# Retention followed by a low-rank mixer: the recurrent state in 64-token steps, on quarter tiles of the TensorE array

## The chip, the cores and the metric

The kernel runs on one core of a Trainium2 chip. A core has a TensorE (PE, matrix multiply; its weight loads are listed as PEld), a VectorE (DVE), a ScalarE (ACT), a GpSimd (POOL) and a SyncE (SP), each with its own queue of instructions, and 16 DMA engines. Matrix products land in PSUM, which VectorE and ScalarE read; everything else lives in SBUF. The metric is the time of one execution on the device in microseconds (us).

## What is computed

Inputs: q, k, v of shape (8 batches, 8 heads, 576 tokens, 64), and the weights of a mixer. The computation, cut to what matters:

```
scores = q @ k^T / sqrt(64)                      # per batch and head, 576 x 576
ret    = scores * gamma_h^(i-j)  for j <= i, else 0
attn   = ret @ v                                 # (8, 8, 576, 64)
x      = attn, heads side by side                # (8, 576, 512)
h      = (x^T @ U @ V)^T                         # U: 576 x 32, V: 32 x 576, along the tokens
u      = x + h
out    = u + relu(u @ w_ch1) @ w_ch2             # 512 -> 2048 -> 512
```

Since gamma^(i-j) = gamma^i * gamma^-j, the kernel scales v's rows by gamma^-j beforehand and the result's rows by gamma^i afterwards. What is between is causal linear attention: within a block of tokens masked scores times v, and for everything earlier q times a running state S, the sum of k^T v over earlier tokens (a 64x64 matrix for each head).

## The kernel before

**Pairs and chunks.** Batches are taken in four pairs (`pr`). The 1152 tokens of a pair make nine chunks of 128 (`NI = 9`); chunk `J = 4` holds the last 64 tokens of the even batch in partitions 0 to 63 and the first 64 of the odd batch in partitions 64 to 127. The first pair has code of its own (`startup`, `first_stretch`, functions ending in `_u` and `_J`), which the change leaves alone but for two memsets. "Later pairs" are pairs 1 to 3.

**One chunk.** q and k come by DMA as float32 (`load`), are cast to bf16 (`cast_qk`: k on VectorE at L244, q on ACT at L246), v is scaled on POOL (`scale_v`, L255), and SP issues a DMA that transposes q and k (`xbar`, L263); casts, scaling and transpose together are `prep`. The attention of a chunk is

- `SC`: eight matmuls k^T q of 64 rows by 128 columns, one for each head, into the PSUM tile psc (two banks; the two heads of a pair stand in different banks);
- `mask`: one VectorE multiply of psc by a triangle, to ret in SBUF (L286);
- `RV`: eight matmuls ret times v into po (two banks); `QS`: eight matmuls q times the state (64 rows), added into po;
- `XS`: one VectorE multiply of po by gamma^i, to x (L326);
- `ST`: four matmuls k^T v, which add to the state that stays in the PSUM tile pss; `Scopy`: one ACT copy of it to bf16 (s_sb, L349), which the next chunk's QS reads.

In `attn_items` a chunk makes two items: A (SC, QS, mask) and Bf (RV, XS, ST, Scopy). The odd batch of a pair starts with an item of its own, SJ, for the state of chunk J's second half.

**The order.** The whole program is in an order written out by hand: each engine gets its instructions as the Python code issues them. The main work of a batch is `y1_items` (L481: 16 feature tiles of u @ w_ch1, four matmuls for each PSUM tile, and after each tile a Relu on ACT at L486 that takes it to SBUF) and then `y2_items` (L515: for each chunk 16 matmuls into one PSUM tile, then the add of u on VectorE at L504 and a store). For an even batch (`par = 0`, four chunks) a Y1 item is one tile of 512 columns; for an odd one (five chunks) it is two tiles, of 384 and 256 columns. In the odd batch of the first pair the two are 512 and 128. All these tiles, and those of Y2, go round the three buffers of `ps_big`.

`merge` goes through the main items, whose costs it knows, and puts the items of two fills between them at equal distances: the attention of the next batch and its mixer (`attn_items` + `mixer_items`) over the first 0.82 of the main cost, and the loads and preps (`aux_items`) over the first 0.62 or 0.58. In the loop b is the batch whose main work runs: with b even (2, 4, 6) the fill is the odd batch of the same pair, with b odd (3, 5) the even batch of the next pair, and the last batch (b = 7) has none. A first merge, ahead of the loop, runs what is left of batch 1's Y1 and the Y2 of batches 0 and 1, and fills in pair 1's even batch.

[...]

Of the kernel before, what the change touches and what calls it, by code (L numbers as in the profile page):

```python
# [9 lines left out]
FP32 = mybir.dt.float32  # L10
BF16 = mybir.dt.bfloat16
AF = mybir.ActivationFunctionType
ALU = mybir.AluOpType


def merge(main, *fills, leads=(0.82, 0.64)):

    total = sum(c for c, _ in main)
    queues = []
    for fill, lead in zip(fills, leads):  # L20
        n = len(fill)
        queues.append([((k + 0.5) / n * lead * total, fn) for k, fn in enumerate(fill)])
    done = 0.0
    for cost, fn in main:
        for q in queues:
            while q and q[0][0] <= done:
                q.pop(0)[1]()
        fn()
        done += cost
    for q in queues:  # L30
        for _, fn in q:
            fn()


@with_exitstack
def kernel(
# [11 lines left out]
    nc = tc.nc  # L48

    B, H, S, D = q.shape  # L50
# [9 lines left out]
    J = 4  # L60
# [28 lines left out]

    ident = consts.tile([P, P], BF16, name="ident")  # L90
    tri = consts.tile([P, P], BF16, name="tri")
    triJ = consts.tile([P, P], BF16, name="triJ")
    triU = consts.tile([P, 2, P], BF16, name="triU")
    iotaU = consts.tile([P, 2, P], FP32, name="iotaU")
    posU = consts.tile([P, 4, 2, H], FP32, name="posU")
# [18 lines left out]
    def early_consts():  # L114
        make_identity(nc, ident)
        nc.gpsimd.memset(lnb, math.log(scale))
        nc.gpsimd.iota(
            posU, pattern=[[2 * P, 4], [1, 2], [0, H]], base=0, channel_multiplier=2,
            allow_small_or_imprecise_dtypes=True,
        )  # L120
        nc.gpsimd.iota(
            iotaU, pattern=[[-1, 2], [1, P]], base=0, channel_multiplier=-2,
            allow_small_or_imprecise_dtypes=True,
        )
        nc.gpsimd.iota(
            pos, pattern=[[P, NI], [0, H]], base=0, channel_multiplier=1,
            allow_small_or_imprecise_dtypes=True,
        )
        make_upper_triangular(nc, tri, val=1.0, diag=True)
        for h in range(H):  # L130
            nc.vector.memset(lngt[:, :, h], lng[h])
        nc.vector.tensor_scalar_add(posU[:, 2:4], posU[:, 2:4], -float(4 * P - HALF))
        nc.vector.tensor_tensor(
            out=posU.rearrange("p u j h -> p (u j) h"),
            in0=lngt[:, 0:8, :], in1=posU.rearrange("p u j h -> p (u j) h"), op=ALU.mult)
        nc.scalar.activation(out=vscaleU, in_=posU, func=AF.Exp, bias=lnb, scale=-1.0)
        nc.vector.tensor_scalar(
            out=triU[0:HALF], in0=iotaU[0:HALF], scalar1=0.0, scalar2=None, op0=ALU.is_ge)
        nc.vector.tensor_scalar(
            out=triU[HALF:P], in0=iotaU[HALF:P], scalar1=-float(P), scalar2=None,  # L140
            op0=ALU.is_ge)
        nc.vector.tensor_scalar_add(pos[:, J + 1:NI, :], pos[:, J + 1:NI, :], -float(S))
        nc.vector.tensor_scalar_add(pos[HALF:P, J, :], pos[HALF:P, J, :], -float(S))
        nc.vector.tensor_tensor(out=lngt, in0=lngt, in1=pos, op=ALU.mult)
        nc.scalar.activation(out=qscale, in_=lngt, func=AF.Exp, bias=0.0, scale=1.0)
        nc.scalar.activation(out=vscale, in_=lngt, func=AF.Exp, bias=lnb, scale=-1.0)
        nc.vector.tensor_copy(out=triJ, in_=tri)
        nc.vector.memset(triJ[0:HALF, HALF:P], 0.0)
        nc.vector.memset(U_E[:, J, :], 0.0)
        nc.vector.memset(U_O[0:HALF, 0, :], 0.0)  # L150
        nc.vector.tensor_copy(out=fan, in_=ident[0:R, None, 0:R].to_broadcast([R, 4, R]))
        nc.vector.tensor_copy(out=swap[:, 0:HALF], in_=ident[:, HALF:P])
        nc.vector.tensor_copy(out=swap[:, HALF:P], in_=ident[:, 0:HALF])
        nc.vector.memset(V4[:, 0:HALF], 0.0)
        nc.vector.memset(V4[:, HALF + S:], 0.0)
        nc.vector.memset(sblk, 0.0)
# [109 lines left out]

    st = {}

    def SC(pr, i):
        c = ch[pr, i]  # L270
        qkT = c["qkT"]
        psc = ps_sc.tile([P, 2, NHP, P], FP32, tag="psc", name="psc")
        for hp in range(NHP):
            for hl in range(2):
                r = slice(hl * HALF, (hl + 1) * HALF)
                nc.tensor.matmul(  # L276
                    psc[:, hl, hp, :], qkT[r, NHP + hp, :], qkT[r, hp, :],
                    start=True, stop=True,
                )
        c["psc"] = psc  # L280

    def mask(pr, i):
        c = ch[pr, i]
        ret = ret_pool.tile([P, H, P], BF16, tag="ret", name="ret")
        m = triJ if i == J else tri
        nc.vector.tensor_tensor(  # L286
            out=ret.rearrange("p (hp hl) i -> p hl hp i", hl=2), in0=c["psc"],
            in1=m[:, None, None, :].to_broadcast([P, 2, NHP, P]), op=ALU.mult,
        )
        c["ret"] = ret  # L290

    def QS(pr, i):
        c = ch[pr, i]
        if "po" not in c:
            c["po"] = ps_o.tile([P, 2, dm], FP32, tag="po", name="po")
        s_sb = st["s_sb"]
        m = slice(0, HALF) if i == J else slice(0, P)
        for hp in range(NHP):
            for hl in range(2):
                r = slice(hl * HALF, (hl + 1) * HALF)  # L300
                nc.tensor.matmul(  # L301
                    c["po"][m, hl, hp * D:(hp + 1) * D],
                    c["qkT"][r, hp, m], s_sb[r, hp, hl * D:(hl + 1) * D],
                    start=(i != J and hp == 0), stop=True, skip_group_check=True,
                )

    def RV(pr, i):
        c = ch[pr, i]
        if "po" not in c:
            c["po"] = ps_o.tile([P, 2, dm], FP32, tag="po", name="po")  # L310
        first = i in (0, J)
        for hp in range(NHP):
            for hl in range(2):
                h = 2 * hp + hl
                nc.tensor.matmul(  # L315
                    c["po"][:, hl, hp * D:(hp + 1) * D],
                    c["ret"][:, h, :], c["v"][:, h, :],
                    start=(first and hp == 0), stop=True, skip_group_check=True,
                )

    def XS(pr, i):
        c = ch[pr, i]
# [8 lines left out]
            op=ALU.mult,  # L331
        )

    def ST(pr, i):
        c = ch[pr, i]
        if i in (0, J):
            st["S"] = ps_s.tile([P, NHP, P], FP32, tag="pss", name="pss")
        rows = slice(HALF, P) if i == J else slice(0, P)
        vf = c["v"].rearrange("p h d -> p (h d)")
        for hp in range(NHP):  # L340
            nc.tensor.matmul(  # L341
                st["S"][:, hp, :],
                c["qk"][rows, 1, hp * P:(hp + 1) * P], vf[rows, hp * P:(hp + 1) * P],
                start=(i in (0, J) and hp == 0), stop=True, skip_group_check=True,
            )

    def Scopy(pr, i):
        s_sb = s_pool.tile([P, NHP, P], BF16, tag="s_sb", name="s_sb")
        nc.scalar.activation(out=s_sb, in_=st["S"], func=AF.Copy)  # L349
        st["s_sb"] = s_sb  # L350

    def attn_items(pr, par):
        items = []

        def A(i):
            SC(pr, i)
            if i not in (0, J):
                QS(pr, i)
            mask(pr, i)

        def Bf(i):
            RV(pr, i)
            if i == J:
                QS(pr, i)
            XS(pr, i)
            if i not in (J, NI - 1):
                ST(pr, i)
                Scopy(pr, i)

        def SJ():  # L370
            ST(pr, J)
            Scopy(pr, J)

        if par == 1:
            items.append(SJ)
        for i in (range(0, J + 1) if par == 0 else range(J + 1, NI)):
            items.append(lambda i=i: A(i))
            items.append(lambda i=i: Bf(i))
        return items

    def mixer_items(pr, par, split=False):
# [514 lines left out]
    def first_stretch():  # L896
# [58 lines left out]
        unit(3, (2, 3), True)  # L955
        load_w2(0)
        load_w2(2)
        xT = [None] * NCC

        def to_xT(ccs, chunks):  # L960
# [43 lines left out]
            Y1(f, 1)  # L1004
        return rest[6:]

    def idle():
        pass

    with tc.manual_schedule():  # L1010
        early_consts()
        startup()
# [8 lines left out]
        for b in range(2, B):  # L1021
            pr, par = divmod(b, 2)
            fill = []
            if b + 1 < B:
                fill = attn_items((b + 1) // 2, (b + 1) % 2) + mixer_items(
                    (b + 1) // 2, (b + 1) % 2)
            n = 5 if b % 2 == 1 else 4
            aux = aux_items(g, g + n)
            g += n
            merge(y1_items(par) + y2_items(pr, par), fill, aux, leads=(0.82, 0.58))  # L1030

# [1 line left out]
_INS = ['q', 'k', 'v', 'moe_U', 'moe_V', 'moe_w_ch1', 'moe_w_ch2']  # L1033
# [26 lines left out]
```

## Time and profile before

| what | us |
|---|---|
| median of three runs | 333.81 (332.57 to 334.24) |
| the profiled execution's own time | 332.29 |
| its span, first to last instruction | 330.5 |
| its busy time on PE / DVE / ACT / POOL | 317.6 / 136.4 / 136.9 / 77.8 |
| L481 and L515, the main matmuls | 135.8 and 124.5 busy |
| L486, the Relus | 89.6 busy |
| L286, L326, L349: mask, XS, state copy | 29.4, 18.6, 14.3 busy |
| TensorE's granted clock | 1.000 |

How to read the lines. A line of the groups names source line, engine, operation, output<-input, shapes and count; then busy us and mean ns of one; then the idle time of the engine just ahead of these instructions and what ended it. A timeline line gives start and length in us, engine, line, operation, and in brackets the idle time before it. A line of the chain of waits in order of time gives start, length and what the end of the program waited for there, merged over neighbouring instructions of the same line ("x8"). [...]

### The profile page before, as it was taken

The numbers are of one execution on the slowest core, as the hardware profiler recorded it, in microseconds if no ns is written. First come the engines' busy times: TensorE is split into PE (matmuls) and PEld (weight loads), VectorE is DVE, ScalarE is ACT, GpSimd is POOL, SyncE is SP. The second block draws the span as 40 slices with busy tenths as digits, with TensorE's granted clock in tenths as the row PEclk, the third lists the DMA queues.
The fourth block names the chain that finished last, engine by engine and source line by source line (L and its number), as shares of the span: only waits on it lengthen the run. The fifth ranks groups of instructions, "written<-read, shape, count | busy, mean of one in ns | idle before, by whom it ended". The sixth has DMA issues, their size and how long they took to land.

```text
span 330.5 us, 7031 instructions
## 1 busy us (share of the span) xinstructions
PE 317.6 (96%) x2942; PEld 174.0 (53%) x2964; DVE 136.4 (41%) x193; ACT 136.9 (41%) x289; POOL 77.8 (24%) x112
## 2 busy tenths in 40 slices
PE   7899999999999999999999999999999996999996
PEld 2464554555444455467644454467644453467544
DVE  5383554444534254534334354534534342510022
ACT  2547656772200573057700573067700662037400
POOL 5675636022221311131121311131211300110000
DMA  7999999999999399949995499959995011330012
GB/s 210 236 226 257 231 196 191 184 171 198 239 238 193 101 226 172 217 125 170 189 251 136 110 218 181 205 135 193 196 211 158 32 34 33 102 106 2 0 70 91
DMA packets 151311, 53.17 MB, mean 161 GB/s; under 512 B 131984, under 2 KB 148752, under 8 KB 151280
## 3 DMA queue, kind: packets, MB, share of 16 engines
q1 hardware_dynamic: 144512, 40.40, 68.0%
q0 software_dynamic: 6768, 12.32, 14.9%
q8 instruction: 23, 0.38, 0.6%
q14 instruction: 8, 0.07, 0.1%
HBM read 36.85 MB, written 9.44 MB: 140 GB/s over the span
## 4 chain that ended last, share of the span: by engine, by line
PE 91%; DMA 3%; DVE 2%; issue 1%; SPq 1%; ACT 1%; POOL 0%
PE ps_y L481 38%; PE ps_y L515 37%; PE psc L276 3%; DMA stage_t<-in_q_dram 2%; PE po L315 2%; PE pss L341 2%; PE pss L691 1%; SPq L578 1%; PE ph L422 1%; PE ps_y L526 1%; PE pa L395 1%; PE po L301 1%; DMA qkT<-qk 1%; DVE xt L682 1%; PE po L665 1%
## 5 line engine op out<-in xcount | busy, mean ns | idle before, releaser
L481 PE MATMUL ps_y<-uT,w_sb 128*128 128x512 bf16 (+3 forms) x768 | 135.8, 326 | 0.4 <-DVE uT L702 0.4
L486 ACT ACTIVATE y<-ps_y 128x384 bf16<-128x384 f32 (+2 forms) x192 | 89.6, 489 | 112.2 <-PE ps_y L481 111.6
L515 PE MATMUL ps_y<-w_sb,y 128*128 128x512 bf16 x538 | 124.5, 379 | 1.5 <-issue 0.8
L481 PEld LDWEIGHTS <-w_sb 128*128 128x128 bf16 x768 | 69.2, 98 | 47.4 <-issue 1.4
L515 PEld LDWEIGHTS <-y 128*128 128x128 bf16 x560 | 52.2, 98 | 59.8
L504 DVE TENSOR_TENSOR o_sb<-ps_y,u 128x512 f32<-128x512 f32 (+2 forms) x38 | 25.2, 663 | 81.5 <-PE ps_y L515 79.3
L255 POOL TENSOR_TENSOR vt<-stage_t,vscale 128x512 bf16<-128x512 f32 (+1 forms) x29 | 30.2, 1049 | 85.2 <-DMA stage_t<-in_v_dram 74.4
L286 DVE TENSOR_TENSOR ret<-psc,tri 128x1024 bf16<-128x1024 f32 x24 | 29.4, 1224 | 44.1 <-PE psc L276 44.1
L507 POOL DMA_DIRECT2D out_dram<-o_sb x31 | 17.2, 554 | 117.5 <-DVE o_sb L504 111.7
L326 DVE TENSOR_TENSOR xt<-po,qscale 128x512 bf16<-128x512 f32 x27 | 18.6, 690 | 25.7 <-PE po L315 24.4
L428 DVE TENSOR_TENSOR u<-ph,xt 128x1024 bf16<-128x1024 f32 (+3 forms) x24 | 21.8, 951 | 11.0 <-PE ph L422 11.0
L246 ACT ACTIVATE qk<-stage_t 128x512 bf16<-128x512 f32 x27 | 16.9, 624 | 8.0 <-DMA stage_t<-in_q_dram 8.0
L401 ACT ACTIVATE a_sb<-pa 128x128 bf16<-128x128 f32 x8 | 2.2, 277 | 34.8 <-PE pa L395 34.8
L349 ACT ACTIVATE s_sb<-pss 128x512 bf16<-128x512 f32 x24 | 14.3, 596 | 4.7 <-PE pss L341 3.6
L647 DVE TENSOR_TENSOR ret<-psc,triU 128x1024 bf16<-128x1024 f32 x8 | 9.7, 1222 | 11.3 <-PE psc L639 11.3
L244 DVE CAST qk<-stage_t 128x512 bf16<-128x512 f32 x27 | 13.1, 485 | 0.9 <-DMA stage_t<-in_k_dram 0.9
L276 PE MATMUL psc<-qkT 64*128 64x128 bf16 x216 | 10.7, 219 | 2.6 <-DMA qkT<-qk 2.6
L596 POOL CAST qk<-stage_t 128x512 bf16<-128x512 f32 x16 | 9.7, 611 | 11.6 <-DMA stage_t<-in_q_dram 8.4
L276 PEld LDWEIGHTS <-qkT 64*128 64x128 bf16 x216 | 6.1, 94 | 11.8 <-issue 8.0
L315 PEld LDWEIGHTS <-ret 128*128 128x128 bf16 x216 | 9.9, 98 | 4.4
L190 PE MATMUL pw<-ident 128*128 128x512 bf16 x33 | 10.2, 448 | 1.4 <-POOL ident masks.py:199 1.4
L315 PE MATMUL po<-vt,ret 128*128 128x64 bf16 x216 | 10.7, 193 | 0.1
(110 smaller groups left out, 159.8 us busy)
## 6 DMA issues: line engine op xcount, KB each, us to landing
stage_t<-in_k_dram SPq DMA_DIRECT2D x32, 256.0 KB, 4.3
stage_t<-in_q_dram SPq DMA_DIRECT2D x32, 256.0 KB, 5.2
stage_t<-in_v_dram SPq DMA_DIRECT2D x32, 256.0 KB, 5.5
out_dram<-o_sb POOLq DMA_DIRECT2D x31, 256.0 KB, 3.4
w_sb<-in_moe_w_ch_dram POOLq DMA_DIRECT2D x4, 512.0 KB, 7.9
w_sb<-in_moe_w_ch_dram POOLq DMA_DIRECT2D x8, 256.0 KB, 9.0
stage_t<-in_k_dram SPq DMA_DIRECT2D x8, 128.0 KB, 3.7
stage_t<-in_q_dram SPq DMA_DIRECT2D x8, 128.0 KB, 4.4
```

Of the source, the lines that this page charges most:

```text
L246: nc.scalar.activation(out=t[rows, 0, :], in_=c["f", 0][rows].rearrange("p h d -> p (h d)"), func=AF.Copy)
L255: (eng or nc.gpsimd).tensor_tensor(out=c["v"][rows], in0=c["f", 2][rows], in1=vscale[rows, i, :, None].to_broadcast([n, H, D]), op=ALU.mult,)
L276: nc.tensor.matmul(psc[:, hl, hp, :], qkT[r, NHP + hp, :], qkT[r, hp, :], start=True, stop=True,)
L286: nc.vector.tensor_tensor(out=ret.rearrange("p (hp hl) i -> p hl hp i", hl=2), in0=c["psc"], in1=m[:, None, None, :].to_broadcast([P, 2, N ...
L315: nc.tensor.matmul(c["po"][:, hl, hp * D:(hp + 1) * D], c["ret"][:, h, :], c["v"][:, h, :], start=(first and hp == 0), stop=True, skip_gro ...
L326: nc.vector.tensor_tensor(out=xt[:, i, :].rearrange("p (hp hl d) -> p hl hp d", hl=2, d=D), in0=c["po"][:, :, 0:NHP * D].rearrange("p hl ( ...
L428: nc.vector.tensor_tensor(out=st["u", par][:, i0 - base:i0 - base + n, w].rearrange("p s (c d) -> p c s d", c=2), in0=ph[k][:, :, 0:n, :], ...
L481: nc.tensor.matmul(ps[:, 0:n, :], w1_sb[:, cc, f * P:(f + 1) * P], st["uT", par][:, c0:c0 + n, cc, :], start=(cc == 0), stop=(cc == NCC - 1),)
L486: nc.scalar.activation(out=st["y1", par][:, f, c0 * P:(c0 + n) * P], in_=ps[:, 0:n, :].rearrange("p s t -> p (s t)"), func=AF.Relu)
L504: nc.vector.tensor_tensor(out=o_sb[:, 0:n], in0=ps[:, 0:n], in1=st["u", par][:, c, w], op=ALU.add)
L507: (nc.sync if last else nc.gpsimd).dma_start(out=out_flat[r0:r0 + P, w], in_=o_sb[:, 0:n])
L515: nc.tensor.matmul(ps, st["y1", par][:, f, c * P:(c + 1) * P], w2_sb[:, f, :], start=(f == 0), stop=(f == NF - 1),)
```

## The change

It concerns pairs 1 to 3, and reworks the attention of a chunk.

- A chunk is now handled in two steps of 64 tokens. `SC` computes only the two 64x64 blocks on the diagonal: 16 matmuls of 64 rows, 64 output partitions and 64 columns, in the four quarter tiles of the array (row half by the head, output half by the step).
- `ST` computes k^T v for each step by itself, again on quarter tiles (row half by the step, output half by the head), into the second half of the two banks of psc; nothing is accumulated in PSUM, and pss is used no more for it.
- The state is float32 in SBUF (`s_f`). The new function `states` adds each step's sum on VectorE (128x256, PSUM and SBUF to SBUF) and then copies both steps' states to bf16 on ACT.
- `mask` is two VectorE multiplies of 64 partitions by 512, one for each step, into one of two ret tiles kept for good (`retz`), whose other blocks are set to zero once, by POOL, in `first_stretch`.
- `QS` is 16 matmuls on quarter tiles: the first step reads the state after the chunk before, the second that after the chunk's first step.
- The items A and Bf become one `section`: RV of the chunk before, SC of this one, QS of the chunk before, ST, mask and states of this one, XS of the chunk before. Between sections stands an item that does nothing. A batch's attention has 11 items (before 10) for an even batch and 9 (before 9) for an odd one; the last section has only RV, QS and XS. SJ is gone.
- triJ, a second triangle for chunk J, is gone with its two VectorE instructions.
- In the loop's last two bodies the loads and preps are spread over 0.3 of the main cost instead of 0.58. Only the two preps of pair 3's last two chunks are left there, in the body of b = 6.

```diff
-    triJ = consts.tile([P, P], BF16, name="triJ")
+    s_f = consts.tile([P, 2, NHP * D], FP32, name="s_f")
+    retz = []
...
-        nc.vector.tensor_copy(out=triJ, in_=tri)
-        nc.vector.memset(triJ[0:HALF, HALF:P], 0.0)
...
+    HALVES = (slice(0, HALF), slice(HALF, P))
+    SW = NHP * D
+
     def SC(pr, i):
...
-        psc = ps_sc.tile([P, 2, NHP, P], FP32, tag="psc", name="psc")
+        psc = ps_sc.tile([P, 2, 2 * SW], FP32, tag="psc", name="psc")
         for hp in range(NHP):
-            for hl in range(2):
-                r = slice(hl * HALF, (hl + 1) * HALF)
-                nc.tensor.matmul(
-                    psc[:, hl, hp, :], qkT[r, NHP + hp, :], qkT[r, hp, :],
-                    start=True, stop=True,
-                )
+            for t in HALVES:
+                for hl, r in enumerate(HALVES):
+                    nc.tensor.matmul(
+                        psc[t, hl, hp * D:(hp + 1) * D], qkT[r, NHP + hp, t],
+                        qkT[r, hp, t], start=True, stop=True,
+                    )
         c["psc"] = psc
+
+    def ST(pr, i, steps):
+        c = ch[pr, i]
+        for hp in range(NHP):
+            for hl, r in enumerate(HALVES):
+                for t in steps:
+                    nc.tensor.matmul(
+                        c["psc"][r, t, SW + hp * D:SW + (hp + 1) * D],
+                        c["qk"][HALVES[t], 1, hp * P + hl * HALF:hp * P + (hl + 1) * HALF],
+                        c["v"][HALVES[t], 2 * hp + hl, :], start=True, stop=True,
+                    )
 
     def mask(pr, i):
         c = ch[pr, i]
-        ret = ret_pool.tile([P, H, P], BF16, tag="ret", name="ret")
-        m = triJ if i == J else tri
-        nc.vector.tensor_tensor(
-            out=ret.rearrange("p (hp hl) i -> p hl hp i", hl=2), in0=c["psc"],
-            in1=m[:, None, None, :].to_broadcast([P, 2, NHP, P]), op=ALU.mult,
-        )
+        ret = retz[i % 2]
+        for t in HALVES:
+            nc.vector.tensor_tensor(
+                out=ret.rearrange("p (hp hl) i -> p hl hp i", hl=2)[t, :, :, t],
+                in0=c["psc"][t, :, 0:SW].rearrange("p hl (hp i) -> p hl hp i", i=D),
+                in1=tri[t, None, None, t].to_broadcast([HALF, 2, NHP, HALF]), op=ALU.mult,
+            )
         c["ret"] = ret
 
+    def states(pr, i, steps):
         c = ch[pr, i]
+        f = s_f
+        b = s_pool.tile([P, 2, SW], BF16, tag="s_sb", name="s_sb")
+        for t in steps:
+            inc = c["psc"][:, t, SW:2 * SW]
+            if (i, t) in ((0, 0), (J, 1)):
+                nc.vector.tensor_copy(out=f[:, t, :], in_=inc)
+            else:
+                nc.vector.tensor_tensor(
+                    out=f[:, t, :], in0=inc,
+                    in1=f[:, 1 - t, :], op=ALU.add)
+        w = slice(steps[0], steps[-1] + 1)
+        nc.scalar.activation(out=b[:, w, :], in_=f[:, w, :], func=AF.Copy)
+        c["s0"] = st.get("s_sb")
+        c["s1"] = b
+        st["s_sb"] = b
...
+    def QS(pr, i):
+        c = ch[pr, i]
+        steps = (1,) if i == 0 else (0,) if i == J else (0, 1)
+        for hp in range(NHP):
+            for t in steps:
+                for hl, r in enumerate(HALVES):
+                    s_sb = c["s1"][:, 0, :] if t == 1 else c["s0"][:, 1, :]
+                    nc.tensor.matmul(
+                        c["po"][HALVES[t], hl, hp * D:(hp + 1) * D],
+                        c["qkT"][r, hp, HALVES[t]], s_sb[r, hp * D:(hp + 1) * D],
+                        start=False, stop=True, skip_group_check=True,
+                    )
...
     def attn_items(pr, par):
+        chunks = list(range(0, J + 1) if par == 0 else range(J + 1, NI))
         items = []
...
+        def section(n):
+            if n > 0:
+                RV(pr, chunks[n - 1])
+            if n < len(chunks):
+                i = chunks[n]
+                steps = (1,) if i == J else (0,) if i == NI - 1 else (0, 1)
+                SC(pr, i)
+            if n > 0:
+                QS(pr, chunks[n - 1])
+            if n < len(chunks):
+                ST(pr, i, steps)
+                mask(pr, i)
+                states(pr, i, steps)
+            if n > 0:
+                XS(pr, chunks[n - 1])
+
+        for n in range(len(chunks) + 1):
+            items.append(lambda n=n: section(n))
+            if n < len(chunks):
+                items.append(idle)
         return items
...
         unit(3, (2, 3), True)
         load_w2(0)
         load_w2(2)
+        for n in range(2):
+            retz.append(ret_pool.tile([P, H, P], BF16, tag="ret", name="ret"))
+            nc.gpsimd.memset(retz[n], 0.0)
...
-            merge(y1_items(par) + y2_items(pr, par), fill, aux, leads=(0.82, 0.58))
+            merge(y1_items(par) + y2_items(pr, par), fill, aux,
+                  leads=(0.82, 0.58 if b < B - 2 else 0.3))
```

The functions that the diff leaves out here (the old QS, RV's flags, the old ST, Scopy, A, Bf and SJ) are only removed or moved; `idle` does nothing.

More of the change, by code (lines that the diff above doesn't have):

```diff
@@ L32, in merge, with idle @@
             fn()
+def idle():
+    pass
 @with_exitstack
@@ L290, in mask @@
         c["ret"] = ret
-    def QS(pr, i):
+    def states(pr, i, steps):
         c = ch[pr, i]
[L294 to L305, printed above, removed]
+        f = s_f
[13 more added lines that the diff above has]
+        st["s_sb"] = b
@@ L307, in RV @@
     def RV(pr, i):
         c = ch[pr, i]
-        if "po" not in c:
-            c["po"] = ps_o.tile([P, 2, dm], FP32, tag="po", name="po")
-        first = i in (0, J)
+        c["po"] = ps_o.tile([P, 2, dm], FP32, tag="po", name="po")
         for hp in range(NHP):
@@ L317, in RV @@
                     c["ret"][:, h, :], c["v"][:, h, :],
-                    start=(first and hp == 0), stop=True, skip_group_check=True,
+                    start=(hp == 0), stop=True, skip_group_check=True,
                 )
+    def QS(pr, i):
[10 more added lines that the diff above has]
+                    )
     def XS(pr, i):
@@ L332, in XS @@
         )
[L334 to L350, printed above, removed]
     def attn_items(pr, par):
+        chunks = list(range(0, J + 1) if par == 0 else range(J + 1, NI))
         items = []
[L355 to L378, printed above, removed]
+        def section(n):
[17 more added lines that the diff above has]
+                items.append(idle)
         return items
@@ L1005, in first_stretch @@
         return rest[6:]
-    def idle():
-        pass
     with tc.manual_schedule():
```

## The prediction

> **What bounds the kernel now.** I read the page's first two parts, then the chain of waits in order of time, then the groups by form and the timelines of ACT and PE.
>
> ```profile
> span 330.5 us, 7031 instructions
> PE 317.6 (96%) x2942; PEld 174.0 (53%) x2964; DVE 136.4 (41%) x193; ACT 136.9 (41%) x289; POOL 77.8 (24%) x112
> ```
>
> TensorE is busy all the time, so its time per chunk counts. The chain (start, us, what) shows that time directly:
>
> ```profile
> 28.16 0.24 PE psc L730 x8
> ...
> 33.29 0.35 PE psc L639 x16
> ...
> 153.08 2.17 PE ps_y L481 x16
> 155.25 0.33 PE psc L276 x8
> 155.58 0.12 PE po L301 x8
> 155.70 2.28 PE ps_y L481 x16
> 157.98 0.23 PE po L315 x8
> 158.21 0.22 PE pss L341 x4
> ...
> 273.62 3.08 DMA qkT<-qk
> ```
>
> The 16 matmuls of L481 take 2.28 behind 64-row matmuls and 2.17 behind 128-row ones: leaving the 64-row form costs 0.10. L276's eight run in pairs (four of 0.056, as L341's four in 0.22) and pay another 0.10 on entry. L301's eight, 64 columns each, are four pairs of 0.03. The last line is TensorE waiting for the last chunk's transposed q and k.
>
> ```profile
> L739 DVE TENSOR_TENSOR ret<-psc,tri 64x512 bf16<-64x512 f32 x2 | 1.4, 682 | 1.0 <-PE psc L730 1.0
> L428 DVE TENSOR_TENSOR u<-ph,xt 128x256 bf16<-128x256 f32 x2 | 0.8, 419 | 0.7 <-PE ph L422 0.7
> L486 ACT ACTIVATE y<-ps_y 128x512 bf16<-128x512 f32 x80 | 47.7, 596 | 65.2 <-PE ps_y L481 64.7
> L486 ACT ACTIVATE y<-ps_y 128x384 bf16<-128x384 f32 x48 | 23.5, 489 | 46.9 <-PE ps_y L481 46.9
> ```
>
> The first two rows price the new VectorE steps, the others the Relus that free PSUM for TensorE. Two timeline stretches give ACT's spacing, and how the old copy follows its matmuls:
>
> ```profile
> 262.67 0.62 ACT L246 ACTIVATE qk<-stage_t 128x512 bf16<-128x512 f32 x1
> 263.19 0.59 ACT L486 ACTIVATE y<-ps_y 128x512 bf16<-128x512 f32 x1
> 263.67 0.60 ACT L349 ACTIVATE s_sb<-pss 128x512 bf16<-128x512 f32 x1
> ```
>
> ```profile
> 158.04 0.39 PE L341 MATMUL pss<-vt,qk 128*128 128x128 bf16 x4
> 158.53 0.60 ACT L349 ACTIVATE s_sb<-pss 128x512 bf16<-128x512 f32 x1
> ```
>
> ACT starts a new instruction 0.52 after a cast from SBUF. The old state copy starts 0.10 after the matmuls it reads: it blocks ACT for nothing.
>
> **Part 1: TensorE per chunk.** Before, a pair of batches costs 9 scores of 0.33, 8 QS of 0.12, 9 RV of 0.23, 8 ST of 0.22 and 9 exits of 0.10, which is 8.66; chunk J's state (0.33 instead of 0.22, an exit) and J's late QS (0.24 instead of 0.12, an exit) add 0.43. Together 9.1. After, there are eleven sections: 9 RV of 0.23; nine scores, now four groups of four 64x64 tiles, 64 columns each; nine QS and nine ST of four groups each; 11 exits. No row has four such tiles at 64 columns. L639 has four tiles at 128 columns: 0.35 for four groups, as 0.056 each plus entry. L730 has two tiles at 64 columns: 0.24 for four groups, 0.03 each plus entry. I take L730's pitch, since L639's 0.056 is also what 128 columns alone take: scores 2.16, QS and ST 0.125 each (2.25), RV 2.07, exits 1.10, two entries of 0.12 for last sections: 7.8. Saved 1.27 a pair, **-3.8** for three. The other bound, 0.056 a group, adds 108 times 0.026, 2.8 a pair: +4.6 in all.
>
> [...]
>
> **Part 2: the last two casts.** Their items come after 3 and 8 Relu items of the seventh body instead of 5 and 14. Each issues a VectorE cast (0.42), an ACT cast (0.62), a POOL scaling (1.05) and one transpose on SP, whose queue holds nothing else there until 285.5. The last one is issued about 266.6 (256.84, eight items of 0.864, sections and stalls) and lands a median 4.3 later, near 271; its scores come near 273.4. The 3.08 wait goes: **-3.1**; at worst it stays.
>
> **Part 3: what is new on VectorE and ACT.** A mask was 1.22; now it is two halves of 0.68. Two state steps of 0.42 follow, and only then the copy on ACT. VectorE has room: 1.36 + 0.84 + 0.69 (L326) + 0.42 (cast) is 3.3 us in a section of 4.3 or more. What matters is what is queued behind the copy: ACT takes Relus and copies in program order, and each Relu frees one of three ps_big tiles.
>
> Let E be where a section's last matmul has given way to the next L481. ST's last matmul starts 0.12 before E and lasts 0.19, so masks start at E+0.08, because they read the two banks that ST writes. The masks take 1.28 (L428 pairs overlap by 0.08), the states 0.83, which ends at E+2.14 with starts that follow closely; the copy starts at E+2.19, the next on ACT 0.52 later, and the first Relu is out after 0.60 (512 columns) or 0.49 (384); 0.05 more to reach TensorE. So the first tile after E comes free at E+3.36 or E+3.25, and 0.52 later where a q cast stands right behind the copy.
>
> TensorE needs it after three tiles. Even bodies (2, 4, 6; four matmuls of 512, 0.864 a tile): E+2.59. Odd bodies (3, 5; tiles of 384 and 256 columns, 2.17 for four): E+1.74. First merge (512 and 128): E+1.95. The stalls are 0.77 (1.29 behind a cast), 2.03 behind a cast, and 1.41 (1.93 behind a cast).
>
> Counting from the merge's positions: bodies 2 and 4 have three such sections, two with a cast directly behind: 3.35 each, 6.7. Body 6 has three without: 2.3. Bodies 3 and 5 have four with a cast: 8.1 each, 16.2. The first merge has two: 3.3. Sections followed by fewer than three Relu tiles, and those among L515, cost nothing: there ACT frees no ps_big tile, VectorE's L504 does, and three tiles of 3.45 cover a delay of 3. Nineteen stalls, **+28.6**. Bounds: if masks needn't wait for ST, each starts 0.25 sooner (four QS and four ST groups), -4.8; if neighbouring VectorE steps overlap more, 0.1 each, -1.9.
>
> **Nothing.** triJ's copy and memset (0.19, 0.09) go from a stretch that waits for the first loads. The two memsets of ret on POOL (0.55 for 64x512 at L800, so 0.6 to 2.2 each) delay a v scaling at 49.3 and six weight loads issued from 50.3 to 54.7, which land about 9 later; L515 first runs at 73.5. No DMA is added. If that cover of some 10 us were gone, they'd cost up to 4.4.
>
> **Sum.** The profiled execution took 332.29 (span 330.5 and 1.8 around it): 332.3 - 3.8 - 3.1 + 28.6 = 354.0. The runs' median, 333.81, is 1.5 above it: **355.5**.
>
> **Rivals.**
> A (0.17): the masks don't wait for ST. For it: they read the scores' half only. Against: halves of the same two banks. 28.6 becomes 23.8: 350.7.
> B (0.13): four-tile groups at 64 columns take 0.056, weight loads being shared. For it: L639 shows nothing quicker; against: L730. +8.4: 363.9.
> C (0.10), the other side: the copies don't hold up the Relus, on ACT during L481. It decides where the copy starts by E+1.42 (even bodies) and E+0.68 (odd), or where Relus pass a waiting copy. For it: ACT is 41% busy and the sums fit. Against: the two masks alone end after E+1.3, and every L349 stands in program order. Then 355.5 - 28.6: 326.9. [...]
> D (0.05): the transposes stay late, 358.6.
>
> **Numbers.** The forecast has 0.55 and its own range is 349 to 365 (its bounds, and a run's spread of 0.8). Taking in A and B whole, 346 to 366 leaves out C and little more. A measurement of this kernel tells 0.5% from no change. Slower 0.88 (forecast, A, B, D, less 0.02 for stalls far smaller), same 0.02, faster 0.10.
>
> **What will show it.** Right: TensorE's busy share falls to about 90%; in L481 stretches its idle time ends on ACT's Relu, near 2 us a section in odd bodies and 0.8 to 1.3 in even ones; the state copies show long idle time ended by VectorE, some 2 us after the section; scores, QS and ST together about 0.5 us on the chain; no wait at a transpose in the seventh body. Wrong: copies that start within a microsecond, Relus among them, groups of 0.056, or stalls elsewhere (QS waiting for its state, RV for ret).

## The result: a tenth slower

| | before | after |
|---|---|---|
| median of the runs | 333.31 us (4 runs, 332.57 to 334.24) | 365.61 us (4 runs, 365.35 to 370.38) |
| profiled execution, its span | 332.29, 330.5 | 370.38, 368.4 |
| TensorE's mean granted clock there | 1.000 | 0.977 (in the other three runs 0.990 or 0.991) |

The ratio is 1.100, with a 95% interval of 1.091 to 1.110. The forecast was 355.5, in a range of 349 to 365. The profiled execution is the slowest of the four; where its 5 us over the other three come from is worked out below, under the clock. Line numbers have moved: L481 is now L492 (first main matmuls), L486 is L497 (their Relus), L515 is L526, the masks are L303, the state adds L319, the state copy L323, scores L282, step sums L293, RV L334, QS L347.

The same two groups of instructions, the first main matmuls on TensorE and the state copies on ACT, before and then after (with the first part of the page of after), with the idle time of the engine ahead of them and what ended it:

```profile
L481 PE MATMUL ps_y<-uT,w_sb 128*128 128x512 bf16 (+3 forms) x768 | 135.8, 326 | 0.4 <-DVE uT L702 0.4
...
L349 ACT ACTIVATE s_sb<-pss 128x512 bf16<-128x512 f32 x24 | 14.3, 596 | 4.7 <-PE pss L341 3.6
```

```profile
PE 327.3 (89%) x3660; PEld 177.7 (48%) x3660; DVE 158.0 (43%) x266; ACT 135.3 (37%) x292; POOL 79.8 (22%) x114
...
L492 PE MATMUL ps_y<-uT,w_sb 128*128 128x512 bf16 (+3 forms) x768 | 143.2, 338 | 33.3 <-ACT y L497 32.6
...
L323 ACT ACTIVATE s_sb<-s_f 128x512 bf16<-128x512 f32 (+1 forms) x27 | 15.7, 582 | 72.1 <-DVE s_f L319 63.6
```

TensorE's first main matmuls stood idle for 0.4 us before and for 33.3 now, and it is the Relu on ACT that they wait for. ACT in turn was idle for 72 us ahead of its 27 state copies, waiting for VectorE's adds; the old copies had 4.7. The next view, the timeline around one section of body 3, shows the chain in order (start, length, engine, line, and in brackets the idle time before and what ended it):

```profile
160.14 1.91 PE L492 MATMUL ps_y<-uT,w_sb 128*128 128x384 bf16 x12
160.28 1.39 DVE L303 TENSOR_TENSOR ret<-psc,tri 64x512 bf16<-64x512 f32 x2 [6.54 <-PE psc L293]
161.70 0.88 DVE L319 TENSOR_TENSOR s_f<-psc,s_f 128x256 f32<-128x256 f32 x2
...
162.68 0.63 ACT L323 ACTIVATE s_sb<-s_f 128x512 bf16<-128x512 f32 x1 [2.79 <-DVE s_f L319]
...
163.22 0.61 ACT L249 ACTIVATE qk<-stage_t 128x512 bf16<-128x512 f32 x1
163.74 1.12 ACT L497 ACTIVATE y<-ps_y 128x384 bf16<-128x384 f32 x3
...
164.26 0.60 PE L492 MATMUL ps_y<-uT,w_sb 128*128 128x256 bf16 x4 [2.21 <-ACT y L497]
```

After the section TensorE does three tiles (12 matmuls, from 160.14) and then has no PSUM buffer. Meanwhile VectorE masks and adds, ACT waits 2.79 for it, copies, casts q, and only at 163.74 starts the Relu that frees the first buffer; TensorE resumes at 164.26. The section itself is cheap, as the chain of waits shows in a stretch where L526 follows:

```profile
78.84 1.08 PE ps_y L526 x5
79.92 0.23 PE po L334 x8
80.15 0.25 PE psc L282 x16
80.40 0.13 PE po L347 x16
80.53 0.13 PE psc L293 x16
80.66 4.42 PE ps_y L526 x20
```

A span lasts until the next piece starts: the first five of L526 take 1.08, 0.216 each, where the page gives a mean of 381 ns for one. RV, scores with their entry, QS and step sums take 0.74, and the exit 0.10 (20 matmuls of L526 at 0.216 are 4.32, and the last line has 4.42). By starts the 16 matmuls of L347, four quarter tiles of 64 columns at a time, go in 0.032 a group. The items of the kernel before took 1.00 for a chunk in the same stretch, their one exit included.

Measured from one body's first main matmul to the next body's, the change added 3.5 us in the first merge, 3.8 in each of bodies 2 and 4, 13.9 and 12.9 in bodies 3 and 5, 0.1 in body 6 (where the late transpose is gone and three waits for the Relu have come) and nothing in body 7, which has no sections.

### The profile page after: what moved, and what is told of

The parts are those of the page before. It is cut to its first block, busy times and chain, and to the rows that moved or that the text cites. A ratio compares the mean times of both kernels' runs of the same rounds, so it can differ in the third digit from the quotient of the medians.

```text
span 368.4 us, 8512 instructions
## 1 busy us (share of the span) xinstructions
PE 327.3 (89%) x3660; PEld 177.7 (48%) x3660; DVE 158.0 (43%) x266; ACT 135.3 (37%) x292; POOL 79.8 (22%) x114
## 4 chain that ended last, share of the span: by engine, by line
PE 66%; DVE 12%; DMA 7%; ACT 6%; issue 4%; SPq 3%; POOL 1%; ACTq 0%; DVEq 0%
PE ps_y L526 31%; PE ps_y L492 24%; DVE ret L303 7%; DMA stage_t<-in_q_dram 4%; DVE s_f L319 4%; ACT y L497 3%; ACT qk L249 2%; PE psc L282 2%; DMA uT<-u 2%; PE po L334 2%; DMA stage_t<-in_v_dram 2%; SPq L589 2%; PE psc L293 1%; PE ph L433 1%; PE po L347 1%
## 5 line engine op out<-in xcount | busy, mean ns | idle before, releaser
L492 PE MATMUL ps_y<-uT,w_sb 128*128 128x512 bf16 (+3 forms) x768 | 143.2, 338 | 33.3 <-ACT y L497 32.6
L526 PE MATMUL ps_y<-w_sb,y 128*128 128x512 bf16 x560 | 126.8, 381 | 0.0
L497 ACT ACTIVATE y<-ps_y 128x384 bf16<-128x384 f32 (+2 forms) x192 | 86.7, 487 | 102.5 <-PE ps_y L492 101.3
L492 PEld LDWEIGHTS <-w_sb 128*128 128x128 bf16 x768 | 72.2, 101 | 89.4 <-issue 42.7
L526 PEld LDWEIGHTS <-y 128*128 128x128 bf16 x560 | 52.8, 98 | 62.0 <-issue 0.8
L303 DVE TENSOR_TENSOR ret<-psc,tri 64x512 bf16<-64x512 f32 x54 | 37.2, 689 | 85.3 <-PE psc L293 84.8
L515 DVE TENSOR_TENSOR o_sb<-ps_y,u 128x512 f32<-128x512 f32 (+2 forms) x38 | 25.1, 662 | 77.1 <-PE ps_y L526 75.0
L323 ACT ACTIVATE s_sb<-s_f 128x512 bf16<-128x512 f32 (+1 forms) x27 | 15.7, 582 | 72.1 <-DVE s_f L319 63.6
L439 DVE TENSOR_TENSOR u<-ph,xt 128x1024 bf16<-128x1024 f32 (+3 forms) x24 | 21.8, 950 | 10.7 <-PE ph L433 10.7
L319 DVE TENSOR_TENSOR s_f<-psc,s_f 128x256 f32<-128x256 f32 x42 | 17.8, 425 | 1.6
L334 PEld LDWEIGHTS <-ret 128*128 128x128 bf16 x216 | 10.4, 100 | 4.6
L334 PE MATMUL po<-vt,ret 128*128 128x64 bf16 x216 | 11.1, 196 | 0.0
L633 ACT ACTIVATE qkT<-pst 128x1024 bf16<-128x1024 bf16 x5 | 6.3, 1255 | 7.6 <-PE pst L622 7.6
```

What stands on the lines that cost most here:

```text
L303: nc.vector.tensor_tensor(out=ret.rearrange("p (hp hl) i -> p hl hp i", hl=2)[t, :, :, t], in0=c["psc"][t, :, 0:SW].rearrange("p hl (hp i) ...
L319: nc.vector.tensor_tensor(out=f[:, t, :], in0=inc, in1=f[:, 1 - t, :], op=ALU.add)
L334: nc.tensor.matmul(c["po"][:, hl, hp * D:(hp + 1) * D], c["ret"][:, h, :], c["v"][:, h, :], start=(hp == 0), stop=True, skip_group_check=True,
L439: nc.vector.tensor_tensor(out=st["u", par][:, i0 - base:i0 - base + n, w].rearrange("p s (c d) -> p c s d", c=2), in0=ph[k][:, :, 0:n, :], ...
L492: nc.tensor.matmul(ps[:, 0:n, :], w1_sb[:, cc, f * P:(f + 1) * P], st["uT", par][:, c0:c0 + n, cc, :], start=(cc == 0), stop=(cc == NCC - 1),)
L497: nc.scalar.activation(out=st["y1", par][:, f, c0 * P:(c0 + n) * P], in_=ps[:, 0:n, :].rearrange("p s t -> p (s t)"), func=AF.Relu)
```

## The experiments

Theory: the state copy stands on ACT behind VectorE's chain and ahead of the Relus, which hold TensorE by the three ps_big buffers. Rivals: the added work on VectorE, or the new tiles, are themselves the cost. All edits are to the changed kernel unless the kernel before is named. Ratios are to the kernel before on the same chip, with 95% intervals.

**The copy taken off ACT.**

```diff
-        nc.scalar.activation(out=b[:, w, :], in_=f[:, w, :], func=AF.Copy)
+        nc.vector.tensor_copy(out=b[:, w, :], in_=f[:, w, :])
```

> The changed kernel with one instruction moved: the state copy to bf16 runs on VectorE, behind the two state adds, instead of on ACT. Theory (the copy holds ACT until VectorE is done, and the Relus behind it hold TensorE through the three ps_big buffers): all 19 waits of L492 for ACT, 35.8 us in the profiled execution, go, and with them the half-speed stretches of TensorE's clock; time 333.3 - 3.8 - 3.1 = 326.4, range 325 to 330. Rival (the extra work on VectorE and its order are what TensorE waits for, and ACT only shows it): the copy adds 27 times 0.42 = 11 us to VectorE, so the time rises from 365.6 toward 375.

Measured: 333.0 us, ratio 1.000 (0.997 to 1.003). VectorE's busy time rose from 158.0 to 168.8 us, no L492 waited for ACT, and 32.6 us went: VectorE's load isn't what TensorE waited for. But the time isn't the 326.4 of the theory. What waits remain are for transfers:

```profile
PEld L492 <- DMA uT<-u: 4.4, 4, 1.9
...
PEld L282 <- DMA qkT<-qk: 2.6, 4, 1.7
```

(who waited for what: us in total, times, longest). The transposes of q and k took a median 5.1 us to land and those of u 6.3, both 4.3 before. The two lines are weight loads; on the matmuls' side the same waits are 2.5 us for uT and 1.9 for qkT, 4.4 of the missing 6.6. That the k casts, now behind the copies on VectorE, send the transposes later is argued from the order, not shown. Nor is it the landing time alone: in the next run the transposes take as long (5.1 and 6.0), and the matmuls wait for them 1.4 us in all. Why this run is above 326.4 stays open in part.

**The copy half a section later, still on ACT.**

```diff
-        nc.scalar.activation(out=b[:, w, :], in_=f[:, w, :], func=AF.Copy)
+        st["copy"] = (b, w)
...
+    def late_copy():
+        b, w = st.pop("copy")
+        nc.scalar.activation(out=b[:, w, :], in_=s_f[:, w, :], func=AF.Copy)
...
-                items.append(idle)
+                items.append(late_copy)
```

> The changed kernel with the state copy still on ACT, but issued half a section later, at the item that does nothing, so two Y1 items or two Y2 items after the section. Theory: when ACT comes to the copy, the adds (done 2.5 us after the section's end) are done or nearly so; waits of L492 for ACT fall below 3 us in all, no half-speed stretch, time 327 to 331. Rival (ACT has no room for 27 copies beside Relus and casts, wherever they stand): waits stay over 15 us, time over 345.

Measured: 328.1 us, ratio 0.989 (0.984 to 0.994), faster than the kernel before. The same copies, on the same engine, now stand where the adds are done:

```profile
149.50 0.68 DVE L362 TENSOR_TENSOR xt<-po,qscale 128x512 bf16<-128x512 f32 x1
```

```profile
149.80 0.62 ACT L330 ACTIVATE s_sb<-s_f 128x512 bf16<-128x512 f32 x1
150.32 0.76 ACT L501 ACTIVATE y<-ps_y 128x384 bf16<-128x384 f32 x2
```

VectorE is already at XS, the step behind the adds, when ACT comes to the copy (L330 here), and the copy has no idle time ahead of it; over the whole run ACT waits 2.2 us for the adds, against 63.6. No first main matmul (L496 here) waits for ACT. So it is the copy's place in ACT's queue that cost the time, neither ACT's load nor the tiles.

**The adds ahead of the masks.**

```diff
-                mask(pr, i)
                 states(pr, i, steps)
+                mask(pr, i)
```

> The changed kernel with the two state adds ahead of the two masks on VectorE, the copy on ACT in its place. Theory: the copy starts 1.42 us sooner (the masks' spacing of 0.70 and 0.72), and each wait shrinks by as much: bodies 2, 4, 6 to 0 to 0.25, odd bodies from 2.4 to 1.0, first merge from 2.3 and 1.8 to 0.9 and 0.4; 10 us in all instead of 35.8, no window of the clock empty enough to halve it; time 334 to 339. Rival (the waits come from the copy and the casts on ACT themselves, not from the chain on VectorE ahead of them): no change, 365.

Measured: 336.6 us, ratio 1.013 (1.010 to 1.017). The waits in body 3 are 1.0 us instead of 2.4, the clock stays at full speed (1.000 in all four executions), and all waits for the Relu, by starts less the matmul's own spacing, come to 10.1 where the expectation had 10. In the timeline (ACT, then TensorE) the copy now waits 1.43 instead of 2.79:

```profile
151.07 0.63 ACT L323 ACTIVATE s_sb<-s_f 128x512 bf16<-128x512 f32 x1 [1.43 <-DVE s_f L319]
```

```profile
152.64 0.60 PE L492 MATMUL ps_y<-uT,w_sb 128*128 128x256 bf16 x4 [0.85 <-ACT y L497]
```

**The same wait put into the kernel before.** Its tiles, its accumulation in PSUM and its items stay; the state reaches ACT by VectorE.

```diff
-        nc.scalar.activation(out=s_sb, in_=st["S"], func=AF.Copy)
+        for _ in range(2):
+            nc.vector.tensor_copy(out=s_f, in_=st["S"])
+        nc.scalar.activation(out=s_sb, in_=s_f, func=AF.Copy)
```

> The kernel before with one thing added: its state goes from PSUM to SBUF by two VectorE copies of 0.69 (one would do), and ACT's copy to bf16 reads that, so ACT's copy waits 1.4 us for VectorE as in the change, with full-size tiles, accumulation in PSUM and the old items. Theory: the copy starts about 1.65 after the section instead of 0.1; the fourth tile of L481 then waits about 1.0 after B0, B1 and B2 of bodies 3 and 5, 0.9 after B0 of the first merge and some 0.2 after SJ and B5 of bodies 2 and 4: 7.7 in all, time 333.3 + 7.7 = 341, range 338 to 344. Rival (ACT, 41% busy, makes up such a wait; what slowed the change is something in its new tiles): 333 to 335.

Measured: 353.0 us, ratio 1.060 (1.055 to 1.065). The waits for the Relu appear where the theory put them, after B0, B1 and B2 of bodies 3 and 5 and in the first merge, 1.4 us each and not 1.0. But they are less than half of the 20 us. Three lines of who waited for whom:

```profile
PE ps_y L484 <- ACT y L489: 8.6, 7, 1.2
PE psc L277 <- DMA qkT<-qk: 4.5, 1, 4.5
PE po L302 <- ACT s_sb L352: 4.4, 8, 0.5
```

In the even bodies the old QS comes half a section behind its state and waits for it (third line, 8 times), and the last transpose of body 6, which the kernel before has late, is later still. Behind that wait of 4.5 us the chain of waits has seven matmuls of L277 in 0.61 us, where the kernel before takes 0.33 for eight, and the execution's mean clock is 0.990: over 352.3 us that is, as an estimate, two stretches of 3.41 us at half speed. Body by body the profiled execution is longer by 1.5 in the first merge, 2.5 in each of bodies 2 and 4, 4.2 in each of 3 and 5, and 6.5 in body 6. The expectation had the mechanism and missed the late QS, the later transpose and the clock. It was no clean isolation, but it shows that the wait needs neither quarter tiles nor sections.

**The other part of the change alone**, in the kernel before:

```diff
-            merge(y1_items(par) + y2_items(pr, par), fill, aux, leads=(0.82, 0.58))
+            merge(y1_items(par) + y2_items(pr, par), fill, aux,
+                  leads=(0.82, 0.58 if b < B - 2 else 0.3))
```

> The kernel before with one line of the change: loads and preps over 0.3 of the main cost in the last two bodies instead of 0.58. Theory: the wait of 3.08 us for the last chunk's transpose goes and nothing takes its place: 333.3 - 3.1 = 330.2, range 329.5 to 331. Rival (the earlier cast on ACT delays Relus in that body as much as it saves): 333, the same as before.

Measured: 329.4 us, ratio 0.992 (0.989 to 0.995): the wait of 3.08 went and nothing took its place. Body 6 is 2.7 us shorter in the profiled execution, and no other body changed. Undoing this part in the changed kernel wasn't tried: with 0.58 the section of chunk 8 (at 11.3 us of main cost) would be issued ahead of its own prep (at 12.0).

**The clock.** In the profiled execution of the change TensorE's granted clock was 0.50 in five stretches of 3.41 us, all in bodies 3 and 5; there the matmuls of L492 with 384 columns start 0.32 apart, elsewhere 0.16. Here is most of body 3 in stretches of that length. Each line gives the stretch, then the busy time of TensorE, its weight loads, VectorE, ACT and GpSimd (with the number of instructions), then the granted clock, DMA share and GB/s:

```profile
148.20:151.60 3.40, 3.40 (x51) 1.93 (x50) 1.19 (x2) 0.82 (x2) 0.98 (x2) 1.00 0.22 77
151.60:155.00 3.40, 1.28 (x10) 0.78 (x8) 2.06 (x5) 1.50 (x4) 1.61 (x2) 1.00 0.20 77
155.00:158.40 3.40, 3.32 (x14) 1.99 (x14) 0.00 (x0) 1.69 (x6) 0.00 (x0) 0.50 0.56 113
158.40:161.80 3.40, 3.40 (x68) 2.57 (x67) 1.48 (x3) 1.06 (x3) 0.00 (x0) 1.00 0.90 192
161.80:165.20 3.40, 1.19 (x10) 0.72 (x9) 1.68 (x4) 2.49 (x6) 0.89 (x1) 1.00 0.08 14
165.20:168.70 3.50, 3.50 (x20) 2.12 (x19) 0.00 (x0) 1.48 (x5) 0.15 (x1) 0.51 1.00 207
168.70:172.10 3.40, 2.58 (x67) 1.76 (x65) 2.47 (x5) 0.47 (x2) 0.77 (x1) 1.00 0.49 90
172.10:175.50 3.40, 1.95 (x15) 1.46 (x15) 0.69 (x2) 3.10 (x8) 0.27 (x1) 1.00 0.36 67
175.50:178.90 3.40, 3.40 (x75) 2.42 (x73) 1.70 (x3) 0.97 (x3) 0.00 (x0) 1.00 0.92 198
178.90:182.30 3.40, 1.15 (x10) 0.84 (x9) 1.45 (x4) 2.56 (x6) 1.04 (x1) 1.00 0.34 71
182.30:185.70 3.40, 3.40 (x57) 2.20 (x56) 1.22 (x2) 0.87 (x2) 0.00 (x0) 0.50 0.99 206
```

Where TensorE (first column) is busy 1.28, 1.19 or 1.15 of a stretch, the next stands at 0.50 or 0.51; after 1.95 it stands at 1.00. The five half-speed stretches start at 155.00, 165.24, 182.31, 247.16 and 264.23, that is 10.24, 17.07, 64.85 and 17.07 apart: 3, 5, 19 and 5 times 3.413. With this execution cut at such multiples, the eight waits of 2.4 us in bodies 3 and 5 sort cleanly: five have 2.25 to 2.41 us in one stretch, and half speed follows each; three are split by a cut, with 1.48, 1.77 and 1.96 at most in one, and 1.00 follows. Only the profiled execution shows its stretches. What the others have is an estimate from their mean clock: 0.977 over 368.4 us is five stretches at half speed, 0.991 over 363.6 is two, and at half of 3.41, some 1.7 us lost in each, three stretches are 5.1, about the 4.8 between the profiled execution and the others. Why the others would have fewer was not shown. To test it, matmuls were put into the waits:

```diff
+            if par == 1 and not by_seg and st.get("tiles") == 3:
+                warm(10)
+            st["tiles"] = st.get("tiles", 9) + 1
```

(`tiles` is set to 0 by each section with a copy.)

> The changed kernel with ten idle matmuls (128x512 of the identity, 0.216 us each, 2.16 in all, into the unused pss bank) put ahead of the fourth tile after each section in the bodies of odd b, where TensorE waits 2.4 us for a Relu. They compute nothing that is used. Theory (an empty wait of 2 us or more within one 3.41 us window of the clock's grid halves the clock for the next window, 5 times in the profiled execution, 2 times in the others, at some 1.7 us each): no half-speed stretch in bodies 3 and 5; time 365.6 - 3.4 = 362.2, range 361 to 363.5, with 21 us more matmul work in it. Rival (the half-speed stretches have another cause, and the waits are no longer than they look): 365.6 or more, half-speed stretches stay.

Measured: 367.8 us, ratio 1.105 (1.100 to 1.110), with a mean clock of 0.999 in the profiled execution, where one half-speed stretch would leave an estimated 0.995 (the other three have 1.000, 0.995 and 1.000). The count of tiles had run on over batches, and three of the eleven fillings stood where TensorE didn't wait, 6.5 us of work. With the count ended at each batch's first Y1:

```diff
                 made.append(1)
+                st["tiles"] = 9
```

> The changed kernel with the ten idle matmuls (2.16 us) at the eight waits of bodies 3 and 5 alone; the run before had them at three more places (start of bodies 3, 5 and 7), where TensorE didn't wait and 6.5 us were added. Theory: no half-speed stretch of the clock, and 367.8 - 6.5 = 361.3, range 360 to 362.8, against 365.6 for the change. Rival (filling the waits costs what the clock gives back): 365 or more.

Measured: 361.9 us, ratio 1.089 (1.084 to 1.093), clock 1.000 in three of the four executions, 0.994 in the slowest. Eighty matmuls more, 17 us of work, made the changed kernel 3.7 us faster, and the slowest of the four (364.0) is faster than the fastest without them (365.4). That is the clock's part of the change's median: a mean clock of 0.991 there is an estimated two stretches of 1.7 us.

**What is left of the good version.** With the late copy TensorE still waits some 1.6 us for transposes of u, by starts 0.6 and 0.7 where body 5 begins and 0.3 where body 6 does. Loads and preps were put over 0.45 of the main cost in the bodies of b = 2 to 5, first with the late copy, then with the copy on VectorE, and over 0.78 with the late copy:

```diff
-                  leads=(0.82, 0.58 if b < B - 2 else 0.3))
+                  leads=(0.82, 0.45 if b < B - 2 else 0.3))
```

> The changed kernel with the copy half a section later (as in the run of 328.1) and, besides, loads and preps over 0.45 of the main cost instead of 0.58 in the bodies of b = 2 to 5. Theory: what is left above 326.4 there is TensorE waiting at the start of bodies 5 and 6 for the transposes of u (0.8, 0.9 and 0.5 us), which are issued right behind a chunk's loads on SP and take 6 us instead of 4.3; with the loads sooner they don't meet: 326 to 327.5. Rival (the DMA engines are full in these bodies whatever the order, so another transfer is late instead): 328 to 330.

> The changed kernel with the copy on VectorE (as in the run of 333.0) and loads and preps over 0.45 of the main cost instead of 0.58 in the bodies of b = 2 to 5. Theory: that run's excess of 6 us over 326.4 is late transposes (waits of 1.8 and 2.8 us at chunks' q and k and at u), whose casts stand behind the copies on VectorE; sooner preps take them off: 327 to 330. Rival (VectorE itself is too full with the copies): no change, 333.

> The changed kernel with the copy half a section later (328.1) and loads and preps over 0.78 of the main cost instead of 0.58 in the bodies of b = 2 to 5. The last loads of a body then stand behind the transposes of u on SP instead of right ahead of them, and loads have longer from landing to cast. Theory: the waits at the starts of bodies 5 and 6 (0.8, 0.9, 0.5) go: 326 to 327.3. Rival (later preps make a chunk's own transpose late: 4.6 us are left for the last one of bodies 2 and 4, and it takes 4.3 to 5.1): 328 to 331, with waits at the scores of chunk 8.

Measured: 336.6 (ratio 1.012, 1.008 to 1.015) and 339.0 (1.018, 1.013 to 1.024) with 0.45, 329.2 (0.989, 0.983 to 0.995) with 0.78. Sooner is worse, and by the mechanism of this study: q casts now stand on ACT before their loads have landed, and hold the Relus. The waits in the first of them:

```profile
ACT qk L249 <- DMA stage_t<-in_q_dram: 22.3, 11, 5.7
...
PE ps_y L496 <- ACT y L501: 5.8, 4, 2.7
```

With 0.58 the late copy has 15.2 us in 7 waits of the first kind and none of the second; with the copy on VectorE and 0.45 they are 29.4 and 9.1.

Later makes no difference that can be told: the intervals of 329.2 and 328.1 overlap, and bodies 2 to 6, which hold all that the edit touches, take 180.1 us in both profiled executions. One wait for u's transpose (1.0, where body 6 starts) stays. The time lies in the rival's range, but not for the rival's reason: the wait of 1.1 at the scores stands in the first merge, whose loads this edit leaves alone, and not at chunk 8 of bodies 2 and 4.

The best version run is the late copy with 0.58, 328.1; it isn't told apart from the kernel before with the one line on leads, 329.4, since the intervals overlap.

## Why the forecast was short of the result

The forecast added up the right terms, found each place and the direction, and came out 10 us short. One term, VectorE's chain ahead of the copy, was sized too small, and one, the clock, was left out.

**TensorE per section (-3.8): right, a little less.** Four-tile groups of 64 columns take 0.032 by starts (L347), L730's pitch (0.032) and not L639's (0.056). Between the late copy and the lead alone the bodies without transfer waits differ by 0.51 (first merge), 0.65 (body 2), 0.49 (body 3) and 0.64 (body 6). A pair's two batches together are then some 1.15 cheaper, against the 1.27 forecast: 3.4 for three pairs.

**The sooner casts (-3.1): right.** Alone they shorten body 6 by 2.7 in the profiled execution and the median by 3.5 (332.96 to 329.44). The rest fits the clock: of the 32 executions of the kernel before that were taken beside the experiments, 18 show a mean clock of 0.994 or 0.995, an estimated one half-speed stretch, with a median of 333.5, and 14 show 0.999 or 1.000, with a median of 331.7; the five with the sooner casts all show 0.999 or 1.000. That the stretch stands behind the wait of 3.08 is argued: no profile of an execution with 0.995 was kept.

**The copy behind VectorE's chain (+28.6): mechanism, number of waits and places right, size short by 7.1.** Nineteen waits were forecast, and nineteen are there, each ahead of the fourth tile. By starts, less the matmul's own spacing, they sum to 35.7: 2.27 and 1.76 in the first merge (forecast 1.93, 1.41), 1.62, 1.69 and 1.17 in bodies 2 and 4 (1.29, 1.29, 0.77), 2.36 to 2.44 in bodies 3 and 5 (2.03), 1.11 to 1.23 in body 6 (0.77). So each is 0.33 to 0.46 longer. The term that failed is VectorE's chain: "the masks take 1.28 ... the states 0.83 ... the copy starts at E+2.19". In body 2's first section (E is, as in the prediction, where the section gives way to the next L492, at 114.50) masks start at E+0.13, the second 0.70 later (0.60 forecast), the first add 0.72 later (0.60), the second 0.53 later (0.44), and the copy starts at E+2.54. The overlap of 0.08 seen between two adds of L428 doesn't appear between the two mask halves, nor before the adds.

**The clock: left out.** The working treated each wait as lost time only. Five of the eight waits of 2.4 us in the profiled execution were followed by a clock of 0.50. Filling the waits took 3.7 us off the median, and five stretches of 1.7 are an estimated 8.5 in the profiled execution. The profiled execution of the kernel before shows no such stretch (clock 1.000), even behind its wait of 3.08, so its page gave no price for one; but it had only that one long wait, and a forecast of eight waits of 2 us and more should have widened the range upward. The forecast also carried over the 1.5 by which the median of the kernel before lies above its profiled execution; by the clocks above that is probably, as an estimate, the kernel's own half-speed stretch, which went with the sooner casts.

With both, and without that 1.5, 354.0 + 7.1 + 8.5 (five stretches) = 369.6, against 370.4 measured; for the median two stretches, 3.4, give 364.5, and 365.6 was measured.

**Rivals.** A, that the masks don't wait for the step sums, is refuted: in body 2's first section the first mask starts 0.06 after the last step sum ends, and in none of the 27 before it. B and D didn't happen. C asked that the copies not hold up the Relus; in the change they did (the Relu at 163.74 above starts right behind a copy and a cast), and the late copy is C brought about on purpose, at 328.1 against the 326.9 worked out for it.

## What to carry to other kernels

In these runs a copy that waited on ACT for VectorE cost what stood behind it in ACT's queue: with 63.6 us of such waits TensorE stood 32.6 us for Relus, and with 2.2 us, the copy half a section later, for none. Ask of every copy moved to a shared engine which Relus, casts or evictions follow it, how many buffers its consumers have left, and when its input will be ready; half a section of distance was worth 37 us here. And a wait on TensorE may have to be counted twice, once as it is and once for the slower clock after it: in the profiled execution of the change five of the eight waits of 2.4 us were followed by half speed, at an estimated 1.7 us each, and none of the shorter ones.

## What the runs showed of the hardware

- TensorE's granted clock: in the profiled execution of the change it was 0.50 in five stretches of 3.41 us and 1.00 in the others. In the 3.41 us ahead of each of the five TensorE was busy 1.16 to 1.29; with the same cuts, stretches with 1.45 (253.99), 1.64 (271.06) and 1.94 (172.07) were followed by 1.00. In the kernel before, 3.40 us with 0.76 busy (from 273.70, most of it the wait for the last transpose) were followed by 1.00. Where the border lies, and what decides it, these runs don't show.
- Two executions of the changed kernel, 370.38 and 365.35 us, have mean clocks of 0.977 and 0.990; taken as half-speed stretches of 3.41 us, these account, as an estimate, for the 5 us between them.
- Ten matmuls of no use in each of eight waits made the changed kernel faster, 365.6 to 361.9.
- The two mask halves on VectorE (L303, partitions 0 to 63 and 64 to 127) start 0.70 apart for a length of 0.68, so they didn't overlap, while two adds of 1.22 on all partitions (L439, at 56.52) started 1.14 apart.
- Four 64x64 tiles of 64 columns ran side by side: in L347 at 80.23 the four matmuls of a group start 0.003 to 0.004 apart, and the 16 take 0.13 on the chain.
